# The hand-over from the attention mixing to the MLP: order of w1's opening split, engine of two low parts, and the buffer of two residual tiles

## The chip, the cores and the metric

The kernel runs on one core of a Trainium2 chip. The metric is the device time of one execution in microseconds, of which the median over several runs is given. The engines are TensorE (PE), VectorE (DVE), ScalarE (ACT), GpSimd (POOL) and SyncE (SP, which issues most of the DMAs here, strictly in its program's order).

## The reference

There are 8 batches of 8 heads, 576 tokens, head size 64. The first half is linear attention with random features: `phi(x) = exp(x·omegaᵀ − |x|²/2 − max)/sqrt(m)` of q and k (m = 128), then `kv = phi(k)ᵀ v`, `z = sum phi(k)`, and `x = phi(q) kv / (phi(q) z + 1e-6)`. Its result, laid out as 8 x 576 tokens of 512 channels, goes into the second half:

```python
h  = x.transpose(0, 2, 1) @ U @ V          # mixing along the tokens, rank 32
u  = x + h.transpose(0, 2, 1)
ch = np.maximum(u @ w_ch1, 0.0) @ w_ch2    # 512 -> 2048 -> 512
out = u + ch
```

U, V, w_ch1 and w_ch2 come as 64-bit floats and are turned into 32-bit ones on the chip.

## The kernel before, in words

**Number format.** Every matmul operand of the MLP is split into a high part (`ScalarE` copies it to the rounded type F32R) and a low part (the difference, by another engine). A product is then three passes: high·high, high·low, low·high. The helper `split(hl, x, rest)` (L700) does this: the cast is on ScalarE (L702), the subtraction (L703) on the engine `rest`, by default GpSimd.

**Stages.** Attention for 16 units runs to about 310 us. For each pair of batches a generator `mixing` then forms u: `prep` splits a tile of x into `mh` and `ml` (L287, L288), a product with U follows (L327), `y` is split (L332, L334), and `spread` and `add` make the tiles of u (L299, L303), which are stored to `u_dram`. In the last mixing the subtractions are on VectorE, and the steps on ScalarE, VectorE and SP are kept in program order.

**Chunks.** The 36 token tiles of u (128 tokens each) are worked in 9 chunks: chunk 0 has six tiles, chunks 1 to 7 four each, the last one two. Chunk 0 needs only tokens of the first pair, so it begins while the last mixing still runs: the loop at L967 walks through the mixer's steps and does one step of `tasks()` (L953) at each, except while `hold` is set (the last two tiles of the mixing's second product). A step is `turn` (a transpose of u on VectorE, L792), or `whole` and `over` (the split of a turned tile into `ux`, and the transpose of the two leftover token tiles), or `Halves(f)` (L767): the split of w1's 128 columns number f into two tiles `wx`. `short` splits the leftovers of two channels tiles. Then comes `whole1` (L837), the first product of the MLP: 12 matmuls of 512 columns, 12 of 256, and `relu`.

**whole_pass** (L982) does chunk 0 for the 16 column blocks f: the second product of f (`second`, L906), the first one of f + 1, and the splits of f + 2. Beside it `each` drives the decoding of the remaining w1 and w2 pieces (raw words fetched by SP into a ring of three buffers `raw`, 4 KB a partition; magnitude on ScalarE, five or three steps on VectorE, an addition on GpSimd), the fetches and turns of chunk 1, and at the end the first operands of chunk 1.

**Chunks 1 to 7** use a scheme with seven products for eight (`products`, L863, L898), 8 pairs of column blocks per chunk. In chunk 1 the weights of the scheme (`Weights`, L717) are formed by sums on VectorE (L706), cast by ScalarE and finished by GpSimd, and stored by SP to `wx_dram` (L754). Later chunks load them back. The second product of the chunk's last block, of chunk 0 too, runs in between the next chunk's first products.

**Residual.** `residual(t)` (L931) loads a tile of u back from `u_dram`: even tiles into a buffer of tag `mag`, odd ones into one of tag `u`, two buffers each. `store(t, po)` (L935) adds the second product to it on VectorE (L938) and sends it out (L939). At the end of chunk 0 the tiles come in the order 4, 5, 0, 1, 2, 3.

**Order.** What goes through `keep` or `tc.keep_in_program_order` stays in program order on its engine; the rest is placed by a planner that simulates the engines' times.

Of the kernel before, what the change touches and what calls it, by code (L numbers as in the profile page):

```python
# [9 lines left out]
F32 = mybir.dt.float32  # L10
# [19 lines left out]
def performer_mlp_kernel(ctx: ExitStack, tc, q, k, v, omega, U, V, w1, w2, out):  # L30
# [7 lines left out]
    nc = tc.nc  # L38
# [3 lines left out]
    DM, DF = w1.shape  # L42
    P = 128
# [14 lines left out]
    def f32(ap):  # L58
        return ap.bitcast(F32)
# [6 lines left out]
    dec = ctx.enter_context(tc.tile_pool(name="dec", bufs=1))  # L66
# [8 lines left out]
    def u_rows(t):  # L75
        c = next(c for c in range(NCH) if t < ends[c])
        return u_dram[c][(t - first[c]) * P : (t - first[c] + 1) * P, :]
# [23 lines left out]
    RB = 3  # L101
# [163 lines left out]
    def advance(gen, n=1, late=False):  # L265
        for _ in range(n):
            if late or left[0] > 0:
                left[0] -= 1
                if next(gen, gen) is gen:
                    return False  # L270
        return True
# [180 lines left out]
    class Queries(Part):  # L452
# [22 lines left out]
        def combine(self, s):  # L475
            eT, kv = self.eT.pop(s), self.keys.kv
            if s == 4:
                bank = ("p_kv", 1) if self.last and self.place else ("p_n", 2)
                self.mixed = ps.tile([P, 2, 2, D1], F32, name="p_n", tag=bank[0], bufs=bank[1])
                for h in range(2):  # L480
                    nc.tensor.matmul(self.mixed[:, h], eT[:, h, :], kv[:, h], start=True, stop=True)
                return
            second = self.second(s)
            if not second:
                self.tiles[s + (not self.last)] = ps.tile([P, 2, 2, D1], F32, name="p_n", tag="p_n", bufs=2)
            pn = self.tiles[s + (not self.last and not second)][:, second]
            for h in range(2):
                nc.tensor.matmul(pn[:, h, :], eT[:, h, :], kv[:, h, s // 5, :], start=True, stop=True)  # L488

        def second(self, s):  # L490
            return self.place if self.last else int(s in (1, 3, 6, 8))
# [121 lines left out]
    for s in range(NR * NT + 7):  # L613
        r, t = divmod(s, NT)
# [85 lines left out]
    def split(hl, x, rest=nc.gpsimd):  # L700

        keep(nc.scalar.copy(out=hl[:, 0], in_=x))  # L702
        keep(rest.tensor_tensor(out=hl[:, 1], in0=x, in1=f32(hl[:, 0]), op=SUBTRACT))  # L703
# [4 lines left out]
    def passes(w, x):  # L708

        return (w[0], x[0]), (w[0], x[1]), (w[1], x[0])  # L710
# [65 lines left out]
    class Chunk:  # L776
# [24 lines left out]

        def whole(self):

            split(self.slot(), self.uT[:, self.turned - 1, :].rearrange("p (k t) -> p k t", k=2))

        def short(self, x, rest=nc.gpsimd):

# [98 lines left out]
        def second(self, fs, gs, begin, end):  # L906


            if begin:
                banks = [("p_m", 1), ("p_kv", 1)] * (self.n > CT) + [("p_n", 2)] * 2 + [("p_q", 2)] * 2  # L910
                self.po = [ps.tile([P, DM], F32, name=n, tag=n, bufs=m) for n, m in banks[: self.n]]

            order = list(range(self.n))
            if end and self.n > CT:
                order = order[CT:] + order[:CT]
            for m, t in enumerate(order):
                po = self.po[(t - CT) % self.n]
                ts = slice(t % CT * P, (t % CT + 1) * P)
                for n, (f, g) in enumerate(zip(fs, gs)):
                    gf = g[t // CT]  # L920
                    for i, (l, r) in enumerate(passes((gf[:, 0, ts], gf[:, 1, ts]), w2s[f])):
                        tc.keep_in_program_order(nc.tensor.matmul(  # L922
                            po, l, r, start=(begin and n + i == 0), stop=(end and n == len(fs) - 1 and i == 2)
                        ))
                        yield
                if end:
                    self.store(t, po)
                    for late in order[m + 4 : m + 5]:
                        self.residual(late)

        def residual(self, t):  # L931
            self.u[t] = (rp if t % 2 else dec).tile([P, DM], F32, name="u", tag="u" if t % 2 else "mag", bufs=2)
            keep(nc.sync.dma_start(out=self.u[t], in_=u_rows(first[self.c] + t)))

        def store(self, t, po):  # L935
# [12 lines left out]
    one = Chunk(0, ahead)  # L948
    ws = {}

    g = None

    def tasks():  # L953
        for i in range(NC):
            one.turn()
            yield
            one.whole()
            one.over(i)
            yield
            if i % 2:  # L960
                one.short(one.left)
        for f in range(2):
            ws[f] = Halves(f)
            yield

    todo = tasks()
    for n, _ in enumerate(mixers[0]):  # L967
        advance(decoder)
# [9 lines left out]
    rp = ctx.enter_context(tc.tile_pool(name="rp", side="right", reuse_waits="tile", bufs=2))  # L978
# [3 lines left out]
    def whole_pass(chunk, g, each):  # L982


        for f in range(NF):
            steps = chunk.second([f], [g], f == 0, f == NF - 1)
            if f + 2 < NF:
                ws[f + 2] = Halves(f + 2)
            if f + 1 < NF:
                places = iter(range(4))  # L990
                g = chunk.whole1(ws.pop(f + 1), lambda: each(f, next(places)))
                for i in places:
                    take(steps, 3 * chunk.n // 2)
                    each(f, i)
                take(steps)
            else:
                each(f, 0)
        return steps
# [3 lines left out]
    def each(f, i):  # L1002
        advance(decoder, 1 + (i < 3), True)
        if 9 <= f < 13 and i == 0:
            nxt.turn()
        if i == 0 and f in (6, 7, 9, 10):
            nxt.fetch()
        if f == 13 and i == 0:
            nxt.prepare()
        if 13 <= f < 15 and i == 1:  # L1010
            nxt.add()
        if f == 14:
            pairs.add()
            one.residual((4, 5, 0, 1)[i])
        if f == NF - 1:
            while advance(decoder, 1, True):
                pass
            while len(pairs.ops) < 5:
                pairs.add()
            while len(nxt.ops) < 3:  # L1020
                nxt.add()
# [86 lines left out]
```

## Time and profile before

| | |
|---|---|
| time, median of 3 runs | 1129.34 us (1129.19 to 1129.35) |
| the profiled execution | 1129.66 us, of which the span is 1127.9 us |
| TensorE busy (matmul) | 1096.9 us, 97% of the span |
| VectorE, ScalarE, GpSimd busy | 683.9, 500.2, 328.1 us (61%, 44%, 29%) |
| granted TensorE clock, mean | 0.983 of full speed |

A row of a timeline has: start in us, duration in us, engine, line of the kernel, operation, output and input with shapes, count, and in brackets the idle time of that engine just ahead and what ended it. A row of the stretches has: the stretch, its length, the busy time (and count) of PE, weight load, DVE, ACT and POOL, the granted TensorE clock, the busy share of the DMA engines and GB/s. Times count from the start of the span.

### The profile page before, as it was taken

The numbers are of one execution on the slowest core, as the hardware profiler recorded it, in microseconds if no ns is written. First come the engines' busy times: TensorE is split into PE (matmuls) and PEld (weight loads), VectorE is DVE, ScalarE is ACT, GpSimd is POOL, SyncE is SP. The second block draws the span as 40 slices with busy tenths as digits, with TensorE's granted clock in tenths as the row PEclk, the third lists the DMA queues.
The fourth block names the chain that finished last, engine by engine and source line by source line (L and its number), as shares of the span: only waits on it lengthen the run. The fifth ranks groups of instructions, "written<-read, shape, count | busy, mean of one in ns | idle before, by whom it ended". The sixth has DMA issues, their size and how long they took to land.

```text
span 1127.9 us, 20592 instructions
## 1 busy us (share of the span) xinstructions
PE 1096.9 (97%) x7105; PEld 986.4 (87%) x7105; DVE 683.9 (61%) x1485; ACT 500.2 (44%) x1405; POOL 328.1 (29%) x339
## 2 busy tenths in 40 slices
PE   8999999999979999989999999999999999999998
PEld 7999889999948887779889999898999989898987
DVE  3899998988967775455743643644644543543421
ACT  4889879798835664333322312212222222222232
POOL 3446547355234554545400100100100100100133
PEclk7999999999969999999999999999999999999999
DMA  7788886673524462374696796796796695685510
GB/s 130 148 152 153 170 183 122 158 139 82 109 70 128 134 165 41 103 262 167 205 273 157 211 263 159 207 266 161 204 269 161 203 270 160 205 256 164 178 57 19
DMA packets 344360, 187.93 MB, mean 167 GB/s; under 512 B 275872, under 2 KB 275872, under 8 KB 344256
## 3 DMA queue, kind: packets, MB, share of 16 engines
q1 hardware_dynamic: 344192, 186.55, 63.0%
q8 instruction: 57, 0.93, 0.4%
q14 instruction: 47, 0.39, 0.1%
q0 software_dynamic: 64, 0.07, 0.0%
HBM read 152.99 MB, written 33.55 MB: 165 GB/s over the span
## 4 chain that ended last, share of the span: by engine, by line
PE 73%; DVE 7%; issue 5%; POOL 5%; ACT 4%; DMA 3%; SPq 2%; POOLq 0%; DVEq 0%; ACTq 0%
PE p_s L898 21%; PE p_n L922 15%; PE p_q L922 13%; PE p_p L850 5%; PE p_n L488 4%; PE p_kv L442 3%; POOL wx L703 3%; PE p_p L530 3%; PE p_p L532 2%; PE p_q L468 2%; PE p_p L531 2%; PE py L327 1%; POOL mag L164 1%; DVE mag L143 1%; DVE mag L140 1%
## 5 line engine op out<-in xcount | busy, mean ns | idle before, releaser
L898 PEld LDWEIGHTS p_s<-ux,wx 128*128 128x128 f32 x2352 | 335.6, 190 | 44.0 <-DVE far L706 3.7
L898 PE MATMUL p_s<-ux,wx 128*128 128x256 f32 x2352 | 346.3, 284 | 6.9 <-DVE far L706 4.1
L922 PE MATMUL p_n<-w2h,g 128*128 128x512 f32 x576 | 196.8, 399 | 0.4 <-ACT g L858 0.4
L922 PE MATMUL p_q<-w2h,g 128*128 128x512 f32 x512 | 191.6, 398 | 0.0
L545 ACT ACTIVATE e<-p_p,nm 128x128 f32<-128x128 f32 x576 | 166.7, 385 | 36.1 <-DVE nm L538 28.3
L411 POOL TENSOR_TENSOR xl<-xT,xh 128x384 fp32r<-128x384 f32 x96 | 101.0, 1069 | 131.9 <-ACT xh L407 113.1
L922 PEld LDWEIGHTS p_n<-w2h,g 128*128 128x128 f32 x576 | 109.8, 191 | 14.9 <-ACT g L858 0.8
L858 ACT ACTIVATE g<-far 128x256 fp32r<-128x256 f32 x112 | 46.8, 418 | 161.8 <-DVE far L706 161.8
L819 POOL TENSOR_TENSOR us<-uT 128x512 f32<-128x512 f32 x14 | 19.1, 1366 | 341.4 <-DVE uT L792 341.4
L706 DVE TENSOR_TENSOR near<-p_s,near 128x256 f32<-128x256 f32 x168 | 70.5, 419 | 73.8 <-PE p_s L898 71.6
L922 PE MATMUL p_n<-w2l,g 128*128 128x512 f32 x288 | 114.8, 399 | 0.0
L538 DVE TENSOR_REDUCE nm<-p_p 128x4 f32<-128x512 f32 x144 | 98.0, 681 | 24.7 <-PE p_p L532 16.9
L703 POOL TENSOR_TENSOR wx<-w1f,wx 128x256 fp32r<-128x256 f32 x88 | 68.2, 791 | 142.8 <-DMA u<-u_dram 83.4
L859 DVE SCALAR_TENSOR_TENSOR g<-p_s,g 128x256 fp32r<-128x256 f32 x56 | 23.8, 425 | 136.2 <-ACT g L858 136.2
L858 ACT ACTIVATE g<-p_s 128x256 fp32r<-128x256 f32 x56 | 21.5, 385 | 187.2 <-PE p_s L898 187.0
L850 PEld LDWEIGHTS p_p<-ux,wx 128*128 128x128 f32 x576 | 89.6, 197 | 16.9 <-POOL wx L703 2.6
L850 PE MATMUL p_p<-ux,wx 128*128 128x256 f32 (+1 forms) x576 | 100.2, 330 | 4.0 <-DVE g L859 2.1
L922 PEld LDWEIGHTS p_q<-w2h,g 128*128 128x128 f32 x512 | 93.7, 191 | 10.3
L922 PE MATMUL p_q<-w2l,g 128*128 128x512 f32 x256 | 101.6, 397 | 0.0
L530 PE MATMUL p_p<-omh,xh 128*128 128x256 f32 x288 | 93.7, 325 | 1.8 <-ACT e L545 1.5
L859 DVE SCALAR_TENSOR_TENSOR g<-far,g 128x256 fp32r<-128x256 f32 x112 | 49.8, 445 | 54.2 <-ACT g L858 54.2
L531 PE MATMUL p_p<-oml,xh 128*128 128x256 f32 x288 | 82.0, 285 | 0.0
(121 smaller groups left out, 1886.5 us busy)
## 6 DMA issues: line engine op xcount, KB each, us to landing
wx<-wx_dram SPq DMA_DIRECT2D x336, 256.0 KB, 3.1
raw<-in_moe_w_ch_dram SPq DMA_DIRECT2D x32, 512.0 KB, 4.0
wx_dram<-wx SPq DMA_DIRECT2D x56, 256.0 KB, 2.5
u_dram<-ut SPq DMA_DIRECT2D x36, 256.0 KB, 2.2
u<-u_dram SPq DMA_DIRECT2D x36, 256.0 KB, 4.3
out_dram<-u SPq DMA_DIRECT2D x36, 256.0 KB, 3.0
kt<-in_k_dram SPq DMA_DIRECT2D x120, 72.0 KB, 2.9
qt<-in_q_dram SPq DMA_DIRECT2D x120, 72.0 KB, 2.8
```

The costliest lines, as they stand in the source:

```text
L411: nc.gpsimd.tensor_tensor(out=self.xl[-1], in0=self.turned, in1=f32(self.xh[-1]), op=ALU.subtract)
L530: nc.tensor.matmul(o, part.xh[g][:, ts], oh, start=True, stop=False)
L531: nc.tensor.matmul(o, part.xh[g][:, ts], ol, start=False, stop=False)
L538: nc.vector.tensor_reduce(out=self.nm[:, :n], in_=self.pp[:, :n], axis=AX.X, op=ALU.max, negate=True)
L545: nc.scalar.activation(out=self.e[:, j, :], in_=self.pp[:, j, :], func=AF.Exp, bias=self.nm[:, j : j + 1])
L703: keep(rest.tensor_tensor(out=hl[:, 1], in0=x, in1=f32(hl[:, 0]), op=SUBTRACT))
L706: keep(nc.vector.tensor_tensor(out=out, in0=a, in1=b, op=op))
L850: nc.tensor.matmul(ph, l, r, start=(cc + i == 0), stop=(cc == NC - 1 and i == 2))
L858: keep(nc.scalar.activation(out=g[:, 0, ts], in_=x, func=AF.Relu))
L859: keep(nc.vector.scalar_tensor_tensor(out=g[:, 1, ts], in0=x, scalar=0.0, in1=f32(g[:, 0, ts]), op0=ALU.max, op1=ALU.subtract))
L898: tc.keep_in_program_order(nc.tensor.matmul(o, l, r, start=(i in (0, 1, 2, 5) and k + j == 0), stop=(k == 1 and j == 2), skip_group_check= ...
L922: tc.keep_in_program_order(nc.tensor.matmul(po, l, r, start=(begin and n + i == 0), stop=(end and n == len(fs) - 1 and i == 2)))
```

## The change

`Halves(0)` moves from behind the loop over the four channel tiles to the first place of `tasks()`. In `whole`, the low parts of the channel tiles 1 and 3 of u are subtracted by VectorE and not by GpSimd. The residual tiles 2 and 3 of chunk 0 are no longer loaded behind the stores of tiles 4 and 5, into the buffers that these leave, but at f = 14, right behind those of tiles 0 and 1, into the two halves of one buffer of the ring of raw weights.

```diff
         def whole(self):
-            split(self.slot(), self.uT[:, self.turned - 1, :].rearrange("p (k t) -> p k t", k=2))
+            i = self.turned - 1
+            split(
+                self.slot(), self.uT[:, i, :].rearrange("p (k t) -> p k t", k=2), nc.vector if i % 2 else nc.gpsimd
+            )
...
                 if end:
                     self.store(t, po)
-                    for late in order[m + 4 : m + 5]:
-                        self.residual(late)
         def residual(self, t):
-            self.u[t] = (rp if t % 2 else dec).tile([P, DM], F32, name="u", tag="u" if t % 2 else "mag", bufs=2)
+            if self.c == 0 and t in (2, 3):
+                if t == 2:
+                    self.more = dec.tile([P, 2, DM], F32, name="more", tag="raw", bufs=RB)
+                self.u[t] = self.more[:, t - 2]
+            else:
+                self.u[t] = (rp if t % 2 else dec).tile([P, DM], F32, name="u", tag="u" if t % 2 else "mag", bufs=2)
             keep(nc.sync.dma_start(out=self.u[t], in_=u_rows(first[self.c] + t)))
...
     def tasks():
+        ws[0] = Halves(0)
+        yield
         for i in range(NC):
...
-        for f in range(2):
-            ws[f] = Halves(f)
-            yield
+        ws[1] = Halves(1)
+        yield
...
         if f == 14:
             pairs.add()
             one.residual((4, 5, 0, 1)[i])
+            if i > 1:
+                one.residual(i)
```

## Rows read from the trace of the kernel before

**Rows 1.** Stretches of ten microseconds, all engines.
```profile
330.00:340.00 10.00, 8.05 (x29) 6.44 (x28) 1.12 (x3) 1.44 (x4) 4.52 (x7) 0.58 0.07 26
...
430.00:440.00 10.00, 7.91 (x33) 6.25 (x32) 6.43 (x11) 3.24 (x6) 4.40 (x4) 0.83 0.17 29
...
480.00:490.00 10.00, 6.69 (x35) 4.85 (x35) 5.24 (x10) 2.59 (x8) 2.53 (x4) 0.93 0.80 294
490.00:500.00 10.00, 9.71 (x56) 8.89 (x57) 5.79 (x14) 4.67 (x14) 6.04 (x8) 0.90 0.92 306
...
510.00:520.00 10.00, 10.00 (x63) 8.94 (x63) 5.73 (x13) 3.64 (x11) 5.36 (x7) 1.00 0.45 168
```

**Rows 2.** Waits of TensorE, 300 to 470: total us, times, longest us.
```profile
PE p_p L850 <- DVE g L859: 2.1, 1, 2.1
PE p_p L850 <- POOL wx L703: 2.0, 1, 2.0
```

**Rows 3.** Waits of TensorE, 460 to 570.
```profile
PE p_s L898 <- DVE far L706: 4.1, 3, 2.2
```

**Rows 4.** Timeline of the hand-over, 317 to 345, all engines.
```profile
318.51 0.70 DVE L792 STREAM_TRANSPOSE uT<-x 128x512 f32<-128x512 f32 x1
...
319.25 0.62 ACT L702 CAST ux<-uT 128x512 fp32r<-128x512 f32 x1 [2.97 <-DVE uT L792]
...
319.78 0.61 ACT L287 CAST mh<-x 128x512 fp32r<-128x512 f32 x1
319.95 1.28 POOL L703 TENSOR_TENSOR ux<-uT,ux 128x512 fp32r<-128x512 f32 x1 [18.84 <-DMA u_dram<-ut]
...
320.42 1.35 DVE L288 TENSOR_TENSOR ml<-x,mh 128x512 fp32r<-128x512 f32 x1 [0.30 <-ACT mh L287]
...
321.83 0.79 PE L327 MATMUL py<-ml,su 128*128 128x512 f32 x1 [0.89 <-DVE ml L288]
...
323.28 0.68 DVE L334 TENSOR_TENSOR y<-py,y 32x512 fp32r<-32x512 f32 x1 [0.90 <-ACT y L332]
...
325.50 1.27 POOL L703 TENSOR_TENSOR ux<-uT,ux 128x512 fp32r<-128x512 f32 x1 [4.27 <-ACT ux L702]
...
327.54 0.65 DVE L303 TENSOR_TENSOR ut<-ph,x 128x512 f32<-128x512 f32 x1
...
331.65 2.78 POOL L703 TENSOR_TENSOR wx<-w1f,wx 128x256 fp32r<-128x256 f32 x4
...
332.43 10.85 PE L850 MATMUL p_p<-ux,wx 128*128 128x512 f32 x46 [1.95 <-POOL wx L703]
...
341.88 0.60 ACT L858 ACTIVATE g<-p_p 128x512 fp32r<-128x512 f32 x1 [1.74 <-PE p_p L850]
```

**Rows 5.** Operations on `ux`, 400 to 520: ns minimum/median/maximum, first and last start.
```profile
L703 DVE TENSOR_TENSOR ux<-us,ux x3: 693/937/1287, 465.6 to 473.4; 128x512 fp32r<-128x512 f32 x3
L703 DVE TENSOR_TENSOR ux<-uT,ux x2: 683/687/691, 457.2 to 478.9; 128x512 fp32r<-128x512 f32 x2
```

**Rows 6.** Timeline of the decoding's last part, 420 to 470.
```profile
431.50 0.66 ACT L123 ACTIVATE low<-raw 128x512 int32<-128x512 uint32 x1 [1.87 <-DMA raw<-in_moe_w_ch_dram]
...
433.42 6.05 PE L850 MATMUL p_p<-ux,wx 128*128 128x512 f32 x24 [2.09 <-DVE g L859]
```

**Rows 7.** Timeline of SP, 330 to 500: DMA issues.
```profile
478.60 0.34 SPq L933 DMA_DIRECT2D u<-u_dram  x1
...
482.99 0.32 SPq L933 DMA_DIRECT2D u<-u_dram  x1
```

**Rows 8.** Timeline of VectorE, 470 to 500.
```profile
481.76 0.69 DVE L938 TENSOR_TENSOR u<-p_q,u 128x512 f32<-128x512 f32 x1 [0.46 <-DMA u<-u_dram]
...
486.00 0.69 DVE L938 TENSOR_TENSOR u<-p_q,u 128x512 f32<-128x512 f32 x1 [2.31 <-DMA u<-u_dram]
```

**Rows 9.** Timeline of TensorE, 464 to 500.
```profile
487.41 0.98 PE L898 MATMUL p_s<-ux,wx 128*128 128x256 f32 x6 [2.23 <-DVE far L706]
...
490.29 1.65 PE L898 MATMUL p_s<-ux,wx 128*128 128x256 f32 x6 [0.45 <-ACT near L876]
```

## The prediction

> **What bounds the kernel now.** The table of the profile comes first: TensorE is busy for 97% of the span, so only stretches in which it waits or runs at the low clock can give time back. The slices of ten microseconds show where these are [rows 1]. In 510 to 520 TensorE is full at granted clock 1.00; in 330 to 340 the clock is 0.58, and in 480 to 500 it is 0.93 and 0.90, with TensorE idle for 3.31 us of the first ten. The waits of TensorE then name what it waited for. Between 300 and 470 us two single waits stand out [rows 2]: the first product of the MLP (L850) on a low part of w1 that GpSimd makes (2.0 us), and one on VectorE's `g` (2.1 us). Between 460 and 570 us the largest are three on `far` (4.1 us) [rows 3]. The first and the last of these stretches are what the change touches. From 565 us to the end TensorE sets the pace, so what is gained before is kept.
>
> **Part 1, the hand-over from the mixing to the MLP.** In the timeline [rows 4] VectorE turns tile 0 of u at 318.51, ScalarE casts it at 319.25, and only behind that, in program order, casts `mh` of the mixing's last tile (319.78). VectorE's `ml` follows at 320.42; it takes 1.35 us, twice the 0.68 us of the 128x512 subtraction below it (323.28), because GpSimd's low part of tile 0 runs beside it from 319.95 to 321.23. The mixing's last product waits for it until 321.83. After the cast and the subtraction of `y` (ends 323.96), GpSimd works without a gap from 325.50: five low parts of u (four tiles and two leftovers, less tile 0), and then w1's opening piece at 331.65. TensorE's first low pass needs that piece, and so starts only at 332.43.
>
> The new order puts `Halves(0)` at the first place of the tasks. Its two casts fall into ScalarE's idle 2.97 us ahead of 319.25; its two subtractions (2.78 us for four, so 0.70 each) into GpSimd's idle 18.84 us ahead of 319.95. Neither issues a DMA. As it takes up the first of the two places ahead of the hold, `turn` of tile 0 keeps its place on VectorE, but tile 0's cast, low part and leftover go behind `y`. So `mh` needs no turn: its cast can be done by about 318, and `ml` starts behind the addition, at about 319.9, and takes 0.68: it ends at 320.6 and not at 321.77, 1.2 us earlier. Against that stand the two GpSimd subtractions beside the two `ml` before it; each can hold one up by at most its own 0.70. That leaves between -0.2 and +1.2; I take +0.7, since they can miss one another in part.
>
> Behind `y` (now at about 323.25) each engine has a new list. GpSimd: tile 0, a leftover, tile 2, that is 3 x 1.28 = 3.8 us before the first group of products can finish, where it had 5 low parts and a quarter of w1 (6.9 us from 325.50). The second leftover and `Halves(1)` come behind and are needed later. VectorE: the two odd low parts, 0.69 us each when alone and up to 1.29 us beside GpSimd [rows 5]. Each stands in VectorE's queue ahead of the next turn and addition and has to wait for its cast (0.62 and two hand-overs, about 0.8 us); what queues behind it are the other turns, the additions that free the PSUM banks of the mixing's output, and their stores. Added up in order, with the turn 0.65, leftover turn 0.35 and addition 0.65: 0.4 + 0.65 + 0.8 + 0.69 + 0.35 + 0.65 + 0.65 + 0.35 + 0.65 + 0.8 (the addition lies in it) + 0.69 = 6.7 us, so tile 3's low part is done at about 329.9. The first group needs it only for its tenth product of twelve; at the low level (1.2 GHz, 0.43 us for 512 columns) products can start 3.8 us before that. What gates their start is then the mixing's product that stands ahead in program order; it needs the fourth addition, done at about 327.8. So the products run from about 328.3, all 48 of them, against 46 left at 332.43: two products are 0.8 us, which makes 3.3 us. If the planner leaves the mixing's two last products ahead of them, as it now has the last one in their middle, the start is behind the sixth addition (about 330.9 + 0.8) and the gain 0.7 us. The mixing's two products cost TensorE 0.4 us each when they come later. **I take 2.5 us for part 1, out of 0 to 4.** The low-clock stretch moves with the start: 46 products take 10.85 us [rows 4] now and the same then.
>
> One rule speaks against the odd low parts on VectorE. The Trainium skill (SBUF — State Buffer, "SBUF: two separate sides") says that a VectorE operation with two SBUF inputs and a GpSimd operation exclude each other for a whole instruction. By that rule both odd low parts could wait out a GpSimd low part, about 1.3 us each. The 1.35 us of `ml` beside GpSimd's 1.28 agrees that one waits for most of the other. By the rule's worst case part 1 would give about 1 us and the sum would be 4.5; the order above puts one of them into a gap of GpSimd, so I stay with 2.5.
>
> Does a start 2.5 us earlier reach the end? The weight decoding behind it fills VectorE, ScalarE and GpSimd until 441 us, and TensorE waits on it once more, 2.09 us at 433.42; the cast behind a late fetch of raw words had waited until 431.50 [rows 6]. This decoding starts behind ScalarE's `g` at 341.88, which waits for TensorE [rows 4]: it moves with it, and so does that stall.
>
> **Part 2, the residual tiles.** Chunk 0 has six output tiles and two buffers each for even and odd u. Tiles 2 and 3 are now fetched only when the output DMAs of tiles 4 and 5 have left the buffer: at 478.60 and 482.99 [rows 7], and SP, which issues in order, keeps w1's stores behind them. VectorE therefore waits 0.46 us at 481.76 and 2.31 us at 486.00 [rows 8]. Behind the second wait stand a sum of w1 and `far`, which frees the PSUM bank of the third product: TensorE waits 2.23 us until 487.41, and again until 490.29 for a copy [rows 9]. The low clock follows: 0.93 and 0.90 over 480 to 500 [rows 1] is 0.7 + 1.0 = 1.7 us of lost full-speed time.
>
> After the change both fetches are issued beside those of tiles 0 and 1, at about 471 to 473, into one buffer of the raw-weight ring. That ring has three; the decoding is through at 441, so nothing holds them up. Cost: two more issues, 0.34 us each, on SP ahead of tile 1's fetch and the stores. Tile 1's sum is made at 478.3, some 2 us after its tile lands now, so the shift stays covered; were it not, VectorE would lose up to 1 us. The third user of the ring after it, `near` of the third pair, needs the buffer at about 496; the two stores are issued long before. What is late next is the copy `near`, 2.9 us behind `far` through VectorE and ScalarE: TensorE will still wait for it by about 1 us. So the two waits go (2.31 + 0.46 = 2.8 us, at least the 2.3 of the long one), and between none and all of the 1.7 us of clock: 2.3 to 4.4. **I take 3.5 us for part 2**, since the idle stretch ahead of the drop loses its longest piece.
>
> **Sum.** 2.5 + 3.5 = 6.0 us, from the profiled execution's 1129.66 to 1123.7. The median of the runs shown is 0.3 us below that execution, so 1123.3.
>
> **Rivals.**
> (a) The front gives nothing: the start is held by additions on VectorE, or what is gained is waited off at the stall of 433.42, should its length grow. For it: VectorE has two more operations with waits ahead of them. Against it: w1's 2.8 us are off the path in any case. Only part 2 is left: 1129.3 - 3.5 = 1125.8.
> (b) The residual part gives nothing, because tile 1's fetch or the stores on SP become what VectorE waits for: 1129.3 - 2.5 = 1126.8. Against it: 2 us of slack.
> (c) Neither shows: the code does what it says, but the start lies where it was, and the freed wait at 486 turns into one for `near`: 1128 to 1130.
> (d) Slower: the decoding between 343 and 441. Many of its operations are not pinned, and a planner orders them by its own simulated times, which change when the stage starts elsewhere. A fetch of raw words that stands on SP behind a fetch of u (there are four) comes late and stalls TensorE, as the one does now: 2.1 us, and the clock of 0.83 over 430 to 440 [rows 1] is another 1.7, so 3.8 us each. From two more such stalls on it is slower than before: 1123.3 + 7.6 = 1130.9, with three 1134.7. For it: TensorE's lead over the decoding is nearly used up there. Against it: the order is fixed by SP's program, which isn't touched.
> (e) The present stall at 433 goes for the same reason: 3.8 us less, 1119.5.
>
> **How the numbers follow.** The forecast 0.61, with its own range of 1120.5 to 1126; (a) 0.13, (b) 0.06, (c) 0.08, (d) 0.08, (e) 0.04. What a measurement here can tell is 0.2%, or 2.3 us, so faster means below 1127.1. Faster: 0.61 + 0.13 + 0.04 and most of (b), 0.82; within: (c) and the rest of (b), 0.10; slower: (d), 0.08. The range of 1119.0 to 1127.2 leaves out (c), (d) and little else.
>
> **What the profile after would show.** Right: GpSimd's w1 subtractions at about 317 and the first L850 products at 328 to 330 without a wait for `wx`; `ml` of the last tile at 0.68 us; residual fetches all issued by 474; no VectorE wait on DMA at L938 for tiles 2 and 3; no clock of 0.5 at 489 to 492. Wrong: a start of L850 after 331.5; a wait for a residual tile elsewhere, or a stall of SP on the new buffer; more than one stall of 2 us between 343 and 441.

## The result, and the profile after

The changed kernel takes 1123.02 us (median), against 1129.34 us before. Its ratio to the kernel before on the same chip is 0.9941, with a 95% interval of 0.9924 to 0.9958: 0.6% faster. The profiled execution took 1124.61 us, of which the span is 1122.8, and so 5.05 us less than the profiled execution of before. That execution was the longest of the four taken of the changed kernel, which matters below.

Attention ends at a slightly different time in every execution, so two profiles are compared from a mark behind it: the first of the two subtractions of `y` in the last mixing (L334), called S0 here. It starts at 313.56 in the profile of before and at 314.00 in that of after. The table cuts the rest of each span at three starts: the second product of chunk 0 (L922 before, L925 after), the first product of chunk 1 (L898, L901), and the first `near` copy of chunk 2.

| us | S0 to second product (hand-over) | chunk 0 | chunk 1 | rest |
|---|---|---|---|---|
| before | 29.56 | 125.57 | 97.27 | 561.9 |
| after | 25.52 | 125.17 | 96.25 | 561.9 |
| difference | -4.04 | -0.40 | -1.02 | 0.0 |

With the later S0 (+0.44) that is the whole difference of the spans, to the tenth of a microsecond that the spans have. So the profile after has 4 us from the hand-over, only 1 us from the residual tiles, and nothing lost or won from chunk 2 on.

The stretches of ten microseconds that answer to [rows 1] (columns as there):

```profile
330.00:340.00 10.00, 10.00 (x50) 8.53 (x49) 4.45 (x10) 4.50 (x10) 4.10 (x5) 0.83 0.28 105
...
430.00:440.00 10.00, 9.28 (x45) 7.52 (x46) 7.78 (x14) 4.03 (x10) 5.11 (x5) 1.00 0.17 26
...
470.00:480.00 10.00, 5.67 (x33) 4.91 (x32) 7.69 (x13) 3.45 (x9) 5.03 (x6) 0.84 1.02 337
480.00:490.00 10.00, 10.00 (x55) 8.99 (x55) 6.34 (x13) 4.13 (x12) 5.37 (x7) 0.82 0.81 263
```

From 330 to 340 TensorE no longer idles and is granted 0.83 instead of 0.58. The drop at the residual tiles is still there, only earlier: 0.84 and 0.82 over 470 to 490, with TensorE idle for 4.33 us of the first ten.

TensorE's waits of after, 300 to 470, against [rows 2]:

```profile
PE p_p L853 <- DVE g L862: 3.0, 2, 2.4
PE ph L299 <- DVE ut L303: 2.9, 2, 2.5
```

And those of 460 to 570, against [rows 3]:

```profile
PE p_s L901 <- DVE far L706: 3.8, 2, 3.2
...
PE p_s L901 <- ACT near L879: 0.7, 1, 0.7
```

The wait for a low part of w1 is gone; at the hand-over TensorE waits longest for one of the mixing's additions instead. The wait for `far` has hardly shrunk: 3.8 us for 4.1, of which 3.2 are now one piece.

The timeline of after at the hand-over, against [rows 4]:

```profile
317.11 1.93 POOL L703 TENSOR_TENSOR wx<-w1f,wx 128x256 fp32r<-128x256 f32 x2 [15.56 <-ACT wx L702]
...
318.36 1.23 DVE L288 TENSOR_TENSOR ml<-x,mh 128x512 fp32r<-128x512 f32 x1
...
320.72 0.67 DVE L288 TENSOR_TENSOR ml<-x,mh 128x512 fp32r<-128x512 f32 x1
...
322.88 0.68 DVE L334 TENSOR_TENSOR y<-py,y 32x512 fp32r<-32x512 f32 x1 [0.52 <-ACT y L332]
...
325.32 0.69 DVE L703 TENSOR_TENSOR ux<-uT,ux 128x512 fp32r<-128x512 f32 x1 [0.69 <-ACT ux L702]
...
326.99 0.69 DVE L303 TENSOR_TENSOR ut<-ph,x 128x512 f32<-128x512 f32 x1
...
327.74 0.80 PE L299 MATMUL ph<-y,sv 128*128 128x512 f32 x1 [2.47 <-DVE ut L303]
...
328.33 3.19 PE L853 MATMUL p_p<-ux,wx 128*128 128x512 f32 x7
...
334.61 5.07 PE L853 MATMUL p_p<-ux,wx 128*128 128x256 f32 x30
```

GpSimd splits w1's opening piece at 317.11, in its idle time, and the products start at 328.33 without waiting for it. What they wait for is the spread ahead of them, which waits 2.47 us for the addition at 326.99, and ahead of that addition stands the odd low part of 325.32.

### The profile page after: what moved, and what is told of

The parts are those of the page before. It is cut to its first block, busy times and chain, and to the rows that moved or that the text cites. A ratio compares the mean times of both kernels' runs of the same rounds, so it can differ in the third digit from the quotient of the medians.

```text
span 1122.8 us, 20593 instructions
## 1 busy us (share of the span) xinstructions
PE 1095.4 (98%) x7105; PEld 986.7 (88%) x7105; DVE 685.8 (61%) x1487; ACT 501.2 (45%) x1405; POOL 326.3 (29%) x337
## 4 chain that ended last, share of the span: by engine, by line
PE 74%; DVE 8%; issue 5%; POOL 4%; ACT 4%; DMA 3%; SPq 2%; POOLq 0%; DVEq 0%; ACTq 0%
PE p_s L901 22%; PE p_n L925 15%; PE p_q L925 13%; PE p_p L853 4%; PE p_kv L442 4%; PE p_n L488 4%; POOL wx L703 3%; PE p_p L530 3%; PE p_p L531 2%; PE p_p L532 2%; PE p_q L468 2%; PE py L327 2%; POOL mag L164 1%; SPq L383 1%; DVE mag L143 1%
## 5 line engine op out<-in xcount | busy, mean ns | idle before, releaser
L901 PEld LDWEIGHTS p_s<-ux,wx 128*128 128x128 f32 x2352 | 336.6, 190 | 42.5 <-issue 3.4
L901 PE MATMUL p_s<-ux,wx 128*128 128x256 f32 x2352 | 346.8, 284 | 6.0 <-DVE far L706 3.8
L925 PE MATMUL p_n<-w2h,g 128*128 128x512 f32 x576 | 196.6, 398 | 0.0
L925 PE MATMUL p_q<-w2h,g 128*128 128x512 f32 x512 | 191.4, 397 | 0.0
L925 PEld LDWEIGHTS p_n<-w2h,g 128*128 128x128 f32 x576 | 109.9, 191 | 14.3
L925 PE MATMUL p_n<-w2l,g 128*128 128x512 f32 x288 | 114.7, 398 | 0.0
L925 PEld LDWEIGHTS p_q<-w2h,g 128*128 128x128 f32 x512 | 93.4, 190 | 10.3
L925 PE MATMUL p_q<-w2l,g 128*128 128x512 f32 x256 | 101.5, 397 | 0.0
L853 PE MATMUL p_p<-ux,wx 128*128 128x256 f32 (+1 forms) x576 | 97.8, 324 | 3.0 <-DVE g L862 3.0
L532 PE MATMUL p_p<-omh,xl 128*128 128x256 f32 x288 | 82.2, 286 | 0.0
```

The source lines that it names most:

```text
L532: nc.tensor.matmul(o, part.xl[g][:, ts], oh, start=False, stop=True)
L853: nc.tensor.matmul(ph, l, r, start=(cc + i == 0), stop=(cc == NC - 1 and i == 2))
L901: tc.keep_in_program_order(nc.tensor.matmul(o, l, r, start=(i in (0, 1, 2, 5) and k + j == 0), stop=(k == 1 and j == 2), skip_group_check= ...
L925: tc.keep_in_program_order(nc.tensor.matmul(po, l, r, start=(begin and n + i == 0), stop=(end and n == len(fs) - 1 and i == 2)))
```

## The experiments

Each ratio is to the kernel before on the same chip, with its 95% interval. "Chunk 1" and "hand-over" are the columns of the table above, read from each kernel's own profile. Kernels with the same edit at the hand-over differ there by up to about 1 us between profiles, and chunk 1 with the old residual fetches takes 96.25 to 97.37 us in four of them.

**The hand-over in its two parts, and the residual part alone.** One kernel has only the new place of `Halves(0)`:

```diff
     def tasks():
+        ws[0] = Halves(0)
+        yield
...
-        for f in range(2):
-            ws[f] = Halves(f)
-            yield
+        ws[1] = Halves(1)
+        yield
```

> Only the new order of the tasks; all low parts of u stay on GpSimd and the residual tiles are fetched as before. My theory (w1's opening piece was what stood between the last mixing and the first product, and with it gone GpSimd's five low parts run in the shadow of the first products): first L850 product at about 328.5 instead of 332.4, one wait of up to 1.5 us for tile 3's low part inside the first group, second product (L922) 2 to 3.5 us earlier, total 2 to 3.5 us below before. Rival (GpSimd's load of u is the gate): it still has five low parts behind y, 6.4 us, so the first products end no more than 1 us earlier and the total falls by under 1 us.

Measured: 1123.69 us, ratio 0.9951 (0.9938 to 0.9965). The hand-over takes 24.03 us, 5.5 less than before and 1.5 less than in the changed kernel. Its timeline on TensorE (S0 is 317.27 here, 3.3 us later than in the profile of after):

```profile
329.61 0.80 PE L299 MATMUL ph<-y,sv 128*128 128x512 f32 x1 [1.06 <-DVE ut L303]
330.20 3.19 PE L850 MATMUL p_p<-ux,wx 128*128 128x512 f32 x7
...
334.04 7.42 PE L850 MATMUL p_p<-ux,wx 128*128 128x512 f32 x41
```

The products begin 12.93 us behind S0, where after has 14.33. GpSimd makes all the low parts of u here, and still the 41 products run through without a wait for one. The gain, 5.5 us by the ratio too, is more than the 2 to 3.5 us that were expected.

A second kernel has only the odd low parts on VectorE:

```diff
         def whole(self):
-            split(self.slot(), self.uT[:, self.turned - 1, :].rearrange("p (k t) -> p k t", k=2))
+            i = self.turned - 1
+            split(
+                self.slot(), self.uT[:, i, :].rearrange("p (k t) -> p k t", k=2), nc.vector if i % 2 else nc.gpsimd
+            )
```

> Only the low parts of tiles 1 and 3 on VectorE; w1's opening piece stays last. My theory: GpSimd ends up to 2.5 us earlier by count, but the second leftover's low part waits for VectorE's longer queue, and w1's piece waits behind it; the first low pass of the MLP starts 0 to 0.8 us earlier and the total changes by less than 0.8 us. Rival (GpSimd's load is the gate): two low parts of 1.27 us less in front of w1's piece, first low pass at about 330, total 2 to 2.5 us below before.

Measured: 1129.33 us, ratio 1.0004 (0.9995 to 1.0013): nothing. The hand-over takes 29.83 us. The wait for `wx` has become longer waits for the additions on VectorE, 300 to 345 us (6.3 us, where before has 3.2 there):

```profile
PE ph L299 <- DVE ut L303: 6.3, 4, 2.5
```

A third has both of these edits, which is part 1 as it was changed:

> Both edits of the hand-over, residual tiles as before. My theory: the second product starts at about 339.5 instead of 343.1, the stall in the decoding near 430 moves with it and stays, the stretch 465 to 500 is that of before 3.5 to 4 us earlier; total 3 to 4.5 us below before. Rival (a) of the prediction: what is gained is waited off in the decoding, total within 1 us of before.

Measured: 1125.21 us, ratio 0.9966 (0.9954 to 0.9978); hand-over 25.69 us, start of the products 14.33 us behind S0, as in the changed kernel. So part 1 shortens the hand-over by 3.9 us. That is the new order's 5.5 less what the odd low parts take back.

A fourth has only part 2:

```diff
                     self.store(t, po)
-                    for late in order[m + 4 : m + 5]:
-                        self.residual(late)
...
+            if self.c == 0 and t in (2, 3):
+                if t == 2:
+                    self.more = dec.tile([P, 2, DM], F32, name="more", tag="raw", bufs=RB)
+                self.u[t] = self.more[:, t - 2]
+            else:
...
             one.residual((4, 5, 0, 1)[i])
+            if i > 1:
+                one.residual(i)
```

> Only the residual tiles 2 and 3 into the raw-weight buffer, hand-over as before. My theory as predicted: VectorE's waits of 2.3 and 0.5 us on the output tiles go, total 2.3 to 4.4 us below before. Rival, after the profile of the whole change: the two extra fetches delay tile 0's sum and w1's stores, the wait of TensorE on far moves ahead by one product and is 3.2 us long, the low clock follows there; total only 0.5 to 1.5 us below before.

Measured: 1126.62 us, ratio 0.9973 (0.9958 to 0.9987). Chunk 1 takes 93.69 us, 3.58 less than before, and the hand-over is that of before (29.22). TensorE waits 1.3 us for `far`.

**The changed kernel once more.** Part 2 gives 3.6 us alone, but 1.0 in the profile of after. Is that the combination, or that execution?

> The changed kernel itself a second time, to see how far its stretches repeat. My theory: counted from the subtraction of y in the mixing (the attention ahead of it varies by 3 us between executions), the second product starts 25.5 us later as in its first profile, 4 us less than before; the residual stretch (chunk 1's start to chunk 2's start) is 93.5 to 96.3 us against 97.3 before, the spread coming from whether the clock falls near 477. Total 1122 to 1124.5. Rival: the 1.0 us of the first profile is all that the residual part gives beside the new hand-over; then that stretch is 96.2 again.

Measured: 1122.41 us, ratio 0.9939 (0.9921 to 0.9956); hand-over 25.20, chunk 1 93.72. It was the execution: the same program has two outcomes of chunk 1, 96.25 us in one profile and 93.72 in the other. VectorE shows where they part. First the execution of after, then this one:

```profile
471.56 0.69 DVE L944 TENSOR_TENSOR u<-p_n,u 128x512 f32<-128x512 f32 x1 [0.85 <-DMA u<-u_dram]
472.17 0.83 DVE L706 TENSOR_TENSOR ws<-w1f 128x256 f32<-128x256 f32 x1
473.11 1.30 DVE L706 TENSOR_TENSOR ws<-ws,w1f 128x256 f32<-128x256 f32 x1
...
476.14 1.19 DVE L703 TENSOR_TENSOR ux<-uT,ux 128x512 fp32r<-128x512 f32 x1
...
477.70 0.42 DVE L706 TENSOR_TENSOR far<-p_s,near 128x256 f32<-128x256 f32 x1
```

```profile
471.68 0.69 DVE L944 TENSOR_TENSOR u<-p_n,u 128x512 f32<-128x512 f32 x1 [0.62 <-DMA u<-u_dram]
472.29 0.41 DVE L706 TENSOR_TENSOR ws<-w1f 128x256 f32<-128x256 f32 x1
472.81 0.77 DVE L706 TENSOR_TENSOR ws<-ws,w1f 128x256 f32<-128x256 f32 x1
...
475.32 0.68 DVE L703 TENSOR_TENSOR ux<-uT,ux 128x512 fp32r<-128x512 f32 x1
...
476.37 0.42 DVE L706 TENSOR_TENSOR far<-p_s,near 128x256 f32<-128x256 f32 x1
```

Both wait for residual tile 0, the first for 0.85 us, the second for 0.62. Behind that 0.23 us, three subtractions and sums take 0.42 + 0.53 + 0.51 = 1.46 us more in the first execution than in the second, and `far` comes that much later. In the first, GpSimd's low parts had begun ahead of VectorE's two slowest operations:

```profile
472.68 1.45 POOL L703 TENSOR_TENSOR ux<-us,ux 128x512 fp32r<-128x512 f32 x1
...
476.06 0.72 POOL L703 TENSOR_TENSOR wx<-ws,wx 128x256 fp32r<-128x256 f32 x1 [0.36 <-ACT wx L702]
```

They start at 472.68 against 473.11, and at 476.06 against 476.14. In the second execution VectorE's `ux` starts at 475.32, just before GpSimd's second low part (475.37), and takes 0.68. There it is GpSimd whose low parts stretch, to 1.91 us for two that take 0.72 to 0.74 each alone:

```profile
474.67 1.91 POOL L703 TENSOR_TENSOR wx<-ws,wx 128x256 fp32r<-128x256 f32 x2
```

The second execution is not free of it either: its sum of 0.77 us at 472.81 begins inside a low part of GpSimd's, and the same sum takes 0.43 us in the profile of after where nothing runs beside it:

```profile
496.12 0.43 DVE L706 TENSOR_TENSOR ws<-ws,w1f 128x256 f32<-128x256 f32 x1
```

The Trainium skill (SBUF — State Buffer, "SBUF: two separate sides") says that of such a pair the one that starts first keeps the shared port for its whole instruction. The traces agree, and closely: VectorE's slowed operation ends when the low part ahead of it has ended and its own time alone has passed, less 0.14 us. For the sum at 473.11 that is 472.68 + 1.45 + 0.43 - 0.14 = 474.42, and it ended at 474.41; for `ux` it is 476.06 + 0.72 + 0.68 - 0.14 = 477.32, and it ended at 477.33. The 16 other pairs of this kind between 315 and 565 us of the profile of after (a subtraction of GpSimd's begun at least 0.08 us ahead, with over 0.15 us left) fit to 0.01 us as well.

TensorE then waits for `far` in the execution of after:

```profile
478.27 2.90 PE L901 MATMUL p_s<-ux,wx 128*128 128x256 f32 x12 [3.23 <-DVE far L706]
```

The 12 products behind that wait take 2.90 us, where six take 0.88 at other places: the granted clock is 0.50 over them, the lower of its two levels. In the second execution the wait is 1.3 us.

**Taking tile 0's wait away.** The changed kernel with all six residual fetches one expert block earlier, where the queue is empty:

```diff
+        if f == 13:
+            one.residual((4, 5, 0, 1)[i])
+            if i > 1:
+                one.residual(i)
...
         if f == 14:
             pairs.add()
-            one.residual((4, 5, 0, 1)[i])
-            if i > 1:
-                one.residual(i)
```

> The changed kernel with all six residual fetches of chunk 0 one column block earlier (f = 13), where SP and the DMA engines have nothing else to do. If the fetches beside w1's stores are what holds VectorE at tiles 5 and 0 (0.6 and 0.6 to 0.9 us) and so TensorE on far, those waits go, the idle time near 475 falls by 1 to 2 us and perhaps the fall of the clock with it: total 1 to 3 us below the changed kernel. Rival: that wait is VectorE's and GpSimd's own queue (operations that run beside each other take twice as long), the fetches hide anyway: within 0.7 us of the changed kernel.

Measured: 1120.36 us, ratio 0.9924 (0.9911 to 0.9937). No residual tile is waited for, and VectorE's sum and `ux` take the times that they have in the second execution:

```profile
470.05 0.68 DVE L944 TENSOR_TENSOR u<-p_n,u 128x512 f32<-128x512 f32 x1
...
471.16 0.78 DVE L706 TENSOR_TENSOR ws<-ws,w1f 128x256 f32<-128x256 f32 x1
...
473.68 0.68 DVE L703 TENSOR_TENSOR ux<-uT,ux 128x512 fp32r<-128x512 f32 x1
```

Chunk 1 takes 92.85 us, and TensorE's wait for `far` is down to 0.6. The interval of the ratio overlaps that of the changed kernel, so the gain is shown in the profile, not in the time.

**Without the odd low parts.** The changed kernel, in which `whole` leaves all low parts to GpSimd as before:

```diff
         def whole(self):
-            i = self.turned - 1
-            split(
-                self.slot(), self.uT[:, i, :].rearrange("p (k t) -> p k t", k=2), nc.vector if i % 2 else nc.gpsimd
-            )
+            split(self.slot(), self.uT[:, self.turned - 1, :].rearrange("p (k t) -> p k t", k=2))
```

> The changed kernel with the low parts of tiles 1 and 3 back on GpSimd. My theory: the two low parts stand on VectorE ahead of the addition that frees the bank of the mixing's product, and cost the first product 1.4 us (it starts 12.9 and not 14.3 us behind the subtraction of y): total 1 to 2 us below the changed kernel, 7 to 8.5 below before. Rival: the shorter list of GpSimd is what makes the first group finish; then tile 3's low part comes 1.3 us later and the total is 0 to 1.5 us above the changed kernel.

Measured: 1122.12 us, ratio 0.9936 (0.9924 to 0.9948); hand-over 23.23 us, 2.3 less than in the profile of after. Its chunk 1 has the worse outcome again (95.42; tile 0 waited for 0.84 us, `far` 3.2), so the gain in the time, 0.3 us where 1 to 2 were expected, cannot be told from nothing here. With the early fetches (the diff of the kernel before this one) as well:

> Both of the two former edits: low parts on GpSimd and the six residual fetches at f = 13. If both theories hold, the sum: 2 to 4 us below the changed kernel, about 1119.5 to 1121. If only the low parts count, about 1121.5 to 1122; if neither, 1123.

Measured: 1119.00 us, ratio 0.9913 (0.9900 to 0.9926). Chunk 1 takes 92.78 us, as in the other kernel with early fetches. The time is a little below the 1119.5 to 1121 us expected of both edits together.

**Is it the fetch behind tile 0?** On TensorE, VectorE and ScalarE the next kernel has the changed kernel's order; only tile 2's fetch goes out behind tile 1's and not between tiles 0 and 1:

```diff
             one.residual((4, 5, 0, 1)[i])
-            if i > 1:
-                one.residual(i)
+            if i == 3:
+                one.residual(2)
+                one.residual(3)
```

> The changed kernel, in which the fetch of residual tile 2 goes out behind that of tile 1 and not between tiles 0 and 1; nothing else moves, on any engine. Theory: what part 2 loses in some executions begins with tile 0, which lands 4.55 to 4.75 us behind its issue (4.1 before the change) because the fetch of tile 2 follows 0.44 us behind it; VectorE then waits 0.58 to 0.85 us for it and in the worse case meets GpSimd's low part at the next two sums. With only tile 1 a microsecond behind it, tile 0 is added at most 4.3 us behind its issue with a wait under 0.3 us, TensorE waits at most 1.5 us on far, and from chunk 1's first product to chunk 2's first near copy it is 93.0 to 93.8 us in every execution (93.7 or 96.3 with the changed kernel); the time is 1121.0 to 1122.5 us. Rival: the landing depends on the six fetches as a whole, or on the stores to wx_dram around them; tile 0 waits 0.5 to 0.9 us as before and the time stays at 1122.4 to 1123.0 us. Second rival: tile 2 now lands later and its own addition waits, up to 1 us.

Measured: 1121.02 us, ratio 0.9918 (0.9903 to 0.9933). The issues on SP, first of after, then of this kernel (start, time of the issue). Between tiles 0 and 1 both have a store of w1's (`wx_dram`), and this kernel has nothing else there:

```profile
466.75 0.38 SPq L939 DMA_DIRECT2D u<-u_dram  x1
467.19 0.48 SPq L939 DMA_DIRECT2D more<-u_dram  x1
467.76 0.42 SPq L754 DMA_DIRECT2D wx_dram<-wx  x1
468.23 0.42 SPq L939 DMA_DIRECT2D u<-u_dram  x1
468.71 0.42 SPq L939 DMA_DIRECT2D more<-u_dram  x1
```

```profile
465.32 0.38 SPq L939 DMA_DIRECT2D u<-u_dram  x1
465.80 0.43 SPq L754 DMA_DIRECT2D wx_dram<-wx  x1
466.28 0.45 SPq L939 DMA_DIRECT2D u<-u_dram  x1
466.78 0.91 SPq L939 DMA_DIRECT2D more<-u_dram  x2
```

And what VectorE does with tile 0 in this kernel:

```profile
469.60 0.69 DVE L944 TENSOR_TENSOR u<-p_n,u 128x512 f32<-128x512 f32 x1 [0.31 <-DMA u<-u_dram]
```

After adds tile 0 at 471.56, 4.81 us behind its issue; this kernel adds it 4.28 us behind, with a wait of 0.31 us (0.01 above what was expected); its next sums and `ux` take 0.68, 0.77 and 0.68 us. Chunk 1 takes 93.71 us and the wait for `far` is 1.3: the better outcome of the changed kernel (93.72), and no more than that. The second rival did not come: tiles 2 and 3 are not waited for. The same order without the odd low parts:

> The same order of residual fetches in the kernel without the odd low parts (1122.12 us, of which 95.4 us lie between chunk 1's first product and chunk 2's first near copy, with 0.84 us of waiting for tile 0). Theory: tile 0's wait falls under 0.3 us, that stretch to 93.0 to 93.8 us, and the time to 1119.8 to 1121.2 us. Rival: tile 0 lands as late as before and time and stretch stay (1121.5 to 1122.7 us).

Measured: 1120.41 us, ratio 0.9919 (0.9904 to 0.9935). Tile 0 is added 3.88 us behind its issue, without a wait; chunk 1 takes 92.92 us. In both the distance in time to their counterparts is about as forecast, but the intervals of the ratios overlap, and one profile of each does not show that the worse outcome is gone.

Why tile 0 lands late stays open. It landed 4.45 to 4.72 us behind its issue in the four in which the load of tile 2 follows 0.44 us behind it, and 3.36 to 4.44 us in the six in which a store follows there and the next load comes about 1 us behind. That speaks for the load behind it. But the upper end of the six belongs to the kernel with part 1 alone, which has the old order of fetches and where VectorE waits for tile 0 as long as it does with part 2 alone (0.58 us):

```profile
473.54 0.69 DVE L941 TENSOR_TENSOR u<-p_n,u 128x512 f32<-128x512 f32 x1 [0.58 <-DMA u<-u_dram]
```

What is shown is the price: in the four kernels with the early fetches tile 0 is never waited for, and chunk 1 takes 92.8 to 92.9 us.

**The rest of the decoding stall.** To the kernel of 1119.00 us:

```diff
-        if i == 0 and f in (6, 7, 9, 10):
+        if i == 0 and f in (6, 7, 10, 11):
             nxt.fetch()
```

> The kernel without the odd low parts and with the six residual fetches a step earlier (1119.0 us), in which two of chunk 1's four fetches of u are issued a step later each (at the tenth and eleventh expert block instead of the ninth and tenth), so that the last raw weight block of the decoder stands ahead of them in SyncE's queue. Theory: what is left of the decoding stall comes from a raw block that lands late behind a fetch of u; TensorE's two waits there (1.5 us together, 0.9 the longest) go, and the time is 1117.3 to 1118.4 us. Rival: the wait there is for VectorE's own queue (a turn of 0.70 us and a low part of 0.69 us ahead of g), which the order of fetches does not shorten: within 0.4 us of 1119.0. A worse outcome, 1119.5 to 1121, would say that the later fetches of u put the turns into the residual stage.

Measured: 1118.03 us, ratio 0.9902 (0.9885 to 0.9919), the shortest time here and inside the range expected, but by luck, for the theory fell: the wait for `g` was not shortened (1.7 us in two pieces, against 1.5), and ScalarE waits 0.9 us for raw words, against 0.6. The ratio can't be told from the 0.9913 of the kernel that it was made from.

**The low clock at the hand-over.** To the same kernel of 1119.00 us:

```diff
+                    if t > 4:
+                        for _ in range(2):
+                            nc.tensor.matmul(
+                                ps.tile([P, DM], F32, name="fill", tag="p_q", bufs=2), w, xs[t][0], start=True, stop=True
+                            )
...
+            if last and t < 7:
+                for _ in range(3):
+                    nc.tensor.matmul(
+                        ps.tile([P, DM], F32, name="fill", tag="p_q", bufs=2), sv[:, 0:P], ys[1], start=True, stop=True
+                    )
```

> The kernel without the odd low parts and with the six residual fetches a step earlier (1119.0 us), to which 21 matmuls are added whose result nobody reads: two after each of the last four products py of the last mixing tile and three after four of its spreads. Theory: the clock at the hand-over falls because TensorE has little to do while VectorE finishes the mixing (granted 0.68 over 320 to 330 us and 0.81 over 330 to 340 us, so some 5 us worth of full clock missing); with the fill the granted clock there stays above 0.9 and the first product, which begins with VectorE's last addition as before, runs at full speed: 1115.5 to 1118 us. Rival: the clock matters little because the stretch waits for VectorE's relu and for GpSimd's low parts rather than for TensorE; the clock rises and the time stays within 0.6 us of 1119.0. Second rival: the added matmuls stand ahead of products that VectorE waits for, each some 0.24 us at full speed and twice that at the lower clock, and the end of the mixing comes 1 to 3 us later: 1120 to 1122 us.

Measured: 1119.31 us, ratio 0.9913 (0.9897 to 0.9928): no gain. The two stretches of it, and then of the kernel without the fill:

```profile
320.00:330.00 10.00, 7.48 (x21) 4.46 (x20) 9.16 (x17) 3.96 (x8) 5.24 (x6) 0.83 0.33 124
330.00:340.00 10.00, 10.00 (x56) 8.55 (x55) 4.48 (x9) 4.54 (x11) 5.97 (x7) 1.00 0.28 105
```

```profile
320.00:330.00 10.00, 6.33 (x14) 3.50 (x14) 9.17 (x17) 3.96 (x8) 5.23 (x6) 0.68 0.32 120
330.00:340.00 10.00, 10.00 (x48) 8.37 (x47) 3.39 (x7) 3.59 (x10) 5.79 (x7) 0.81 0.28 105
```

The clock rises as meant, but the products begin 14.35 us behind S0 instead of 12.63, since the added matmuls stand ahead of them. The hand-over ends 1.1 us sooner in this profile (23.20 against 24.32), which another kernel without the fill shows too (23.23), and nothing of it is seen in the time. The first rival came true.

## Why the prediction was right, and which of its terms were off

**The direction and the sum were right (1123.3 us forecast, 1123.02 measured); the sizes of its terms were not.** Part 1 gave more than its 2.5 us: 3.8 by its ratio. Part 2 gave 3.0 us by its ratio, and in chunk 1 its 3.5 us in some profiles and 1 to 2 in others. That the sum came within 0.3 us is in part luck: the two errors offset each other in part, and executions of the changed kernel range from 1118.11 to 1125.55 us.

**The split of w1 and the mixing.** As worked out: GpSimd's subtractions at 317.11, the last tile's `ml` at 0.67 us instead of 1.35, and the cost moved to the `ml` before it (1.23 beside GpSimd). From S0, `y` is subtracted 0.84 us earlier, where 0.7 was taken.

**The gate.** Right: the fourth addition gates the start. Forecast at about 328.3 and found at 328.33, it was met in part by chance, since S0 is 0.44 us later there; from S0 the forecast was 14.7 us and the start lies at 14.33. The term mis-sized is the value taken for the start's gain, 2.5 us. The prediction had 3.3 from its own sum and lowered it for the case that two more of the mixing's products stand ahead. They don't: seven products run, then a spread, then eleven. Part 1 measured 3.9 us alone and 4.0 in the profile after. Nor did the low clock only move with the start: from the start of the long run of products to the second product it was granted 0.72 over 10.69 us before and 0.77 over 11.19 us after, in which two more products and two spreads run; they cost 0.5 us and not 0.4 each.

**The odd low parts.** The prediction named their place in VectorE's queue ahead of the turn and addition, and then took the whole order as one. The kernel with the new order alone shows their price: the low part and its wait for the cast (0.69 + 0.69 us at 325.32) are the 1.4 us by which the products start later. What they relieved, GpSimd, TensorE was not waiting for. The long exclusion that the prediction allowed for did not occur here: the two took 0.69 and 0.79 us, and the loss is queueing.

**The decoding stall.** "Moves with it, and so does that stall" was right for the profile of after, against [rows 6]:

```profile
428.19 0.66 ACT L123 ACTIVATE low<-raw 128x512 int32<-128x512 uint32 x1 [2.20 <-DMA raw<-in_moe_w_ch_dram]
...
430.12 4.49 PE L853 MATMUL p_p<-ux,wx 128*128 128x512 f32 x24 [2.39 <-DVE g L862]
```

But the stall is no constant of the program. The kernel in which only a later fetch was moved has the same instructions up to there, and in its profile:

```profile
426.76 0.67 ACT L123 ACTIVATE low<-raw 128x512 int32<-128x512 uint32 x1 [0.62 <-DMA raw<-in_moe_w_ch_dram]
```

The raw words are used 3.97 us behind their issue (422.79) there, 5.55 us in after (422.64); TensorE waits 0.7 us instead of 2.4, and chunk 0 takes 123.51 us instead of 125.17. Rival (d), more such stalls, was not seen. Rival (e), the stall gone, came in part in some profiles, but not for the reason that it gave and not at its price.

**Part 2.** Right: the two waits of [rows 8] are gone, the fetches go out without a stall of SP, the buffer of the ring is free, and the next wait, for `near`, is 0.7 us (about 1 forecast). Small slips: only one new issue stands ahead of tile 1's fetch, the new issues take 0.42 to 0.48 us and not 0.34, and the terms of the range add up to 2.3 to 4.5. The step that failed is "the shift stays covered". It was checked for tile 1, whose fetch is pushed back by a new issue, and tile 1 is never waited for. Tile 0 was not looked at, though it had next to no slack: issued ahead of both new fetches, it was added 4.10 us behind its issue before.

```profile
470.75 0.38 SPq L933 DMA_DIRECT2D u<-u_dram  x1
```

```profile
474.85 0.69 DVE L938 TENSOR_TENSOR u<-p_n,u 128x512 f32<-128x512 f32 x1
```

With part 2 as it was changed it is added 4.5 to 4.8 us behind it, with 0.58 to 0.85 us of waiting. Without that wait chunk 1 is about 0.9 us shorter (the early fetches). In the two profiles with 0.84 and 0.85 us of it, VectorE's next operations also fell behind GpSimd's, and 3.5 us became 1 or 2. In the two kernels with tile 2's fetch moved back the wait was 0.31 us and none; why tile 0 lands late is not settled, as shown above.

**The rivals.** (a), (b) and (c) are excluded by the parts measured alone: 0.9966 (0.9954 to 0.9978) and 0.9973 (0.9958 to 0.9987), neither of which holds 1. What the sum of them would be, 0.9939, is what the changed kernel has.

## What to carry to other kernels

Work taken off an engine pays only if something waits for that engine there: ask for every moved operation what stands behind it in its new queue, as the odd low parts show, which cost 1.4 us on VectorE and freed a GpSimd that was not the gate. A new fetch is checked against its neighbours on both sides, since a load ahead of it with no slack may come later too (here likely, not shown); the place that helped in every profile was an earlier one, where the queue was idle. A single profile of a kernel with such close calls shows one of its outcomes; compare the stage's length over several before explaining it.

## What was not expected of the hardware

**A clock that falls in one execution and not in the next.** With an idle time of 2.09 us at 433.42, before has a granted clock of 0.83 over 430 to 440 [rows 1, 6]; after idles for 2.39 us at the same place and keeps 1.00. The length of the idle time does not decide it alone: 1.85 us at this place was followed by 0.83 in the kernel with part 2 alone, 2.71 us by 1.00 in the changed kernel with early fetches. The 1.7 us per stall, which the prediction counted for it, is thus not a fixed price.

**The landing of one and the same fetch differs by 1.9 us** between the profiles in which the order of fetches up to it is the same (the last raw block is used 3.97 to 5.84 us behind its issue, each time after a wait for it). What decides it was not found. The Trainium skill (DMA: Bandwidth & Descriptors, "Queues, rings and completion order") says that each DMA engine takes a ring's descriptors in order and that a later one may still finish its write first; no run here shows the single engines, and the whole residual fetches landed in the order of their issue (in after at 471.47, 472.13, 473.48 and 474.44).

**The start of the last mixing** moves by 3.7 us between the profiles (S0 from 313.56 to 317.27), more than most of the effects here. The rest behind chunk 1 is the same to 0.1 us in all of them.
